# Batch 0's job list of an attention + gated-FFN kernel in another order, and the last pair of x turned by DMA

## The chip, the cores and the metric

The kernel runs on one core of a Trainium2 chip. The core has five engines that work side by side, each through its own list of instructions in order: TensorE (PE, matmuls; its weight loads, PEld, overlap them), VectorE (DVE), ScalarE (ACT), GpSimd (POOL) and SyncE (SP, which here only issues DMAs). An instruction that needs another engine's result waits at the head of its list, and everything behind it on that engine waits too. The metric is the device time of one execution in microseconds (us).

## What is computed

Four batches of eight heads, 768 tokens, head size 64. Queries and keys are hashed by the signs of six projections; a query attends only to keys with the same hash. The output of the attention, with the heads side by side, is x (3072 x 512), and x goes through a gated FFN with a residual.

```python
q_bits = einsum('bhsd,dk->bhsk', q, proj) > 0          # the same for k
mask = q_bucket[:, :, :, None] == k_bucket[:, :, None, :]
attn = softmax(where(mask, q @ k.T / sqrt(D), -1e9))
x = (attn @ v).transpose(0, 2, 1, 3).reshape(B * S, H * D)
out = x + sigmoid(x @ w_res) * ((gelu(x @ w_gate) * (x @ w_val)) @ w_out)
```

## The kernel before

**Pairs and slots.** Two heads form a pair (p = 0 to 15, four to a batch). A pair's scores are computed in nine slots; a slot (`scores`, L535) is three or two matmuls into a PSUM tile of 1024 columns, `sp` (two buffers), and one exp of 128x1024 on ScalarE (L553). Two slots later, or where the list says so, `values` (L506) multiplies by v, eight matmuls (L515), into `av`. When a head is done, `finish` (L458) divides by the sum on VectorE (L466, L467) and writes x with the tokens on the partitions, `x_tok`. The FFN needs x the other way round, `x_sb`, in four quarters, one a pair. A quarter is turned either by a DMA transpose that SP issues (L470), or on TensorE by `x_turn` (L496): six transposes into PSUM (L499) and copies to `x_sb` by ScalarE and VectorE (L501 to L504).

**The hash inside the matmul.** The six signs stand beside the 64 numbers of each query and key in one row of 71, so that the matmul itself lets only equal hashes through. For that each pair's q and k go through these steps, named here as in the list: `ld` loads it (SP), `tr` transposes it on VectorE (L265), `h` multiplies it by the projections on TensorE (L283, several pairs in one group, four steps: h10 to h13 are group 1, pairs 2 and 3), `tk` turns a group's results on VectorE (L303), `bt` takes the signs (L319; for k of pairs 1 to 3 two of its four instructions are on GpSimd, two on VectorE), `cs` casts the numbers to bf16 beside them on GpSimd (L223 for q, L225 for k), and then either `tp` turns the rows on TensorE, six transposes to a head (L384), with `td` copying them out on VectorE (L393), or `tu` turns them by one DMA transpose (L372). In a name like tp310 the digits are pair, side (0 is q, 1 is k) and head. There are four tiles `nat` for the rows, one for each side of two pairs, and two PSUM banks for turns and hashes.

**v** is loaded by `lv`, cast on GpSimd by `va` (L432, L433) and summed there by `vs` (four instructions, L440 to L444).

**Weights.** `w0` to `w11` each issue one DMA of a slice of the FFN's weights from GpSimd (L208): four times gate and val by turns, then the residual's, then three of the output's. The issue itself occupies GpSimd.

**What sets the order.** Nothing is scheduled by a tool: the order in which the program emits its pieces is the order of every engine. For batch 0 a list written out by hand, `ORDER` (L20), gives it: s and v are the slots' scores and values, fin a `finish`, xt an `x_turn`; the job names are bound to functions in L716 to L766. `FIRST_LOADS` (L17) gives the first loads on SP. Ahead of the list stand fixed pieces for pair 0 and the casts of pair 1 (L626 to L655), among them the cast of pair 1's q, va(0), the cast of pair 1's k and the spreading of the projections over `projw`, in this order on GpSimd. The list ends where x of batch 0 is complete. `BESIDE` (L31) names the jobs that are emitted behind each of the twelve steps m of batch 0's FFN stage (`gate_val`, L570): a step is eight matmuls for gate and eight for val (L566), Gelu on ScalarE (L583) and their product on VectorE (L586). From pair 4 on the jobs are placed by slot numbers (L681 to L826), and the rest of the FFN (`project`, L592: for each of six token blocks four row matmuls by w_res and twelve by w_out, 96 in all, L598 and L614) is spread over the next batch's 36 slots by `mlp_mm` (L831, L851). `HELD`, 16, of them are kept back for the end of a batch, where they fill the time in which x is turned (L857 to L872). In batches 1 and 2 all four quarters of x are turned by DMA; in batch 0 the last two, and in batch 3 the last one, on TensorE.

## Time and profile before

| what | value |
|---|---|
| median of 3 runs | 340.84 us (340.73 to 341.19) |
| the profiled execution's own time | 340.31 us |
| its span, first to last instruction | 338.6 us |
| mean granted TensorE clock | 1.000 |
| busy: PE, DVE, ACT, POOL | 333.2, 216.9, 206.2, 171.9 us |
| first exp of batch 0 | 7.80 us |
| end of batch 0's 36 exps | 44.99 us |
| its FFN stage (gate and val matmuls) | 48.4 to 80 us |
| batches 1 to 3 in slots | 80 to 280 us |
| last batch's FFN stage | 280 us to the end |

In a row of a timeline stand the start, the length of the group, the engine, the line, the operation with out<-in by the program's names, the shapes and a count; in brackets how long the engine was idle before it, and what ended that. A row can hold several instructions, and a length of TensorE is modelled and reaches into the next row, so that one reads such lengths from start to start. Rows of a window (A:B) give the sum of all engines and then PE, PEld, DVE, ACT and POOL, each busy time with its count, the granted clock, the DMA engines' busy share, and GB/s. The chain of work that ended last names at each moment what the end of the program hung on.

### The profile page before, as it was taken

Reading aid. Unit: us, or ns where it says so; the run is one execution under the profiler, and the core shown is the slowest. Engines: PE = TensorE matmul, PEld = TensorE weight load, DVE = VectorE, ACT = ScalarE, POOL = GpSimd, SP = SyncE. Lnnn points to the kernel's source line nnn. Section 1 sums busy time; section 2 is a strip of 40 time slices with the busy share of each in tenths; the row PEclk is TensorE's granted clock in tenths of the full one; section 3 lists DMA queues with packets and bytes.
Section 4 is the critical chain, followed back from the end, with each engine's and each line's share of the span. In section 5 each row is a group of like instructions: output and inputs, shape, how many; then the busy total and the mean of one; then the engine's idle time right before and its main releaser. Section 6 shows DMA issues by size and latency. Waiting matters only on the chain.

```text
span 338.6 us, 7598 instructions
## 1 busy us (share of the span) xinstructions
PE 333.2 (98%) x3058; PEld 203.1 (60%) x3058; DVE 216.9 (64%) x418; ACT 206.2 (61%) x232; POOL 171.9 (51%) x220
## 2 busy tenths in 40 slices
PE   8999999999999999999999999999999999999995
PEld 4667766655666655655666665656566665666444
DVE  6889457574445748888887766887897444343343
ACT  4889963317999952235999982233999984223220
POOL 5879920410665306998999704998998000000000
PEclk9999999999999999999999999999999999999999
DMA  7997897799876634350488832551261420000012
GB/s 211 379 249 169 160 252 128 132 190 199 240 164 187 207 94 99 73 96 0 126 219 204 277 106 62 102 96 28 48 148 39 97 56 33 31 0 2 31 64 94
DMA packets 71459, 43.09 MB, mean 127 GB/s; under 512 B 49536, under 2 KB 68480, under 8 KB 71424
## 3 DMA queue, kind: packets, MB, share of 16 engines
q1 hardware_dynamic: 65008, 37.37, 43.7%
q0 software_dynamic: 6336, 5.24, 10.1%
q8 instruction: 24, 0.39, 0.5%
q14 instruction: 11, 0.09, 0.1%
q10 hardware_dynamic: 80, 0.00, 0.0%
HBM read 29.56 MB, written 6.29 MB: 106 GB/s over the span
## 4 chain that ended last, share of the span: by engine, by line
PE 91%; ACT 4%; DVE 3%; issue 1%; DVEq 0%; ACTq 0%
PE sp L566 35%; PE fps L614 18%; PE sp L542 17%; PE av L515 9%; PE rps L598 6%; ACT hh L553 4%; PE hs L283 2%; DVE hh L586 1%; PE wps L189 1%; PE pt L384 1%; PE hs L330 1%; DVE nat L319 1%; DVE hsum L361 0%; PE pt L499 0%; DVE o L621 0%
## 5 line engine op out<-in xcount | busy, mean ns | idle before, releaser
L553 ACT ACTIVATE e<-sp 128x1024 bf16<-128x1024 f32 x108 | 109.0, 1028 | 8.1 <-PE sp L542 2.8
L357 POOL TENSOR_TENSOR pd<-ld,prow 128x768 f32<-128x768 f32 x48 | 86.1, 1811 | 36.8 <-PE hs L283 32.6
L583 ACT ACTIVATE gt<-sp 128x768 bf16<-128x768 f32 x48 | 38.9, 810 | 89.8 <-PE sp L566 89.8
L542 PE MATMUL sp<-aug,aug 71*128 71x256 bf16 (+1 forms) x384 | 85.5, 325 | 0.1
L614 PE MATMUL fps<-wo,hh 128*128 128x512 bf16 (+2 forms) x312 | 79.5, 362 | 0.0
L566 PE MATMUL sp<-x_sb,wv 128*128 128x512 bf16 (+1 forms) x384 | 70.9, 326 | 0.4 <-DVE hh L586 0.4
L566 PE MATMUL sp<-x_sb,wg 128*128 128x512 bf16 (+1 forms) x384 | 70.9, 326 | 0.1
L586 DVE TENSOR_TENSOR hh<-gt,sp 128x768 bf16<-128x768 bf16 x48 | 45.8, 954 | 39.0 <-PE sp L566 34.2
L515 PEld LDWEIGHTS <-e 128*128 128x128 bf16 x864 | 40.2, 97 | 25.1
L566 PEld LDWEIGHTS <-wv 128*128 128x128 bf16 x384 | 37.6, 98 | 25.5 <-issue 0.8
L566 PEld LDWEIGHTS <-wg 128*128 128x128 bf16 x384 | 36.9, 98 | 25.8 <-issue 1.7
L361 DVE TENSOR_REDUCE hsum<-pd 128x12 f32<-128x768 f32 x48 | 44.4, 943 | 0.5
L515 PE MATMUL av<-va,e 128*128 128x65 bf16 x864 | 43.4, 193 | 0.0
L614 PEld LDWEIGHTS <-hh 128*128 128x128 bf16 x312 | 28.1, 97 | 21.8
L553 ACT ACTIVATE hh<-sp 128x1024 bf16<-128x1024 f32 x36 | 34.5, 1024 | 3.4 <-PE sp L542 3.0
L542 PEld LDWEIGHTS <-aug 71*128 71x128 bf16 x384 | 29.5, 97 | 11.0 <-issue 1.1
L617 DVE SCALAR_TENSOR_TENSOR fps<-th,fps 128x512 f32<-128x512 f32 (+2 forms) x26 | 16.9, 650 | 28.3 <-PE fps L614 27.8
L598 PE MATMUL rps<-wr,x_sb 128*128 128x512 bf16 x96 | 27.1, 379 | 0.0
L494 DVE COPY av<-av 128x390 f32<-128x390 f32 x24 | 13.7, 571 | 19.6 <-PE av L490 19.6
L602 ACT ACTIVATE th<-rps 128x512 f32<-128x512 f32 x24 | 14.3, 594 | 18.5 <-PE rps L598 18.5
L223 POOL TENSOR_SCALAR nat<-ld 128x768 bf16<-128x768 f32 (+1 forms) x16 | 13.0, 813 | 18.6 <-DMA aug<-nat 18.0
L265 DVE STREAM_TRANSPOSE t<-ld 128x768 f32<-128x768 f32 (+1 forms) x24 | 21.9, 925 | 0.1
(77 smaller groups left out, 259.6 us busy)
## 6 DMA issues: line engine op xcount, KB each, us to landing
ldv<-in_v_dram SPq DMA_DIRECT2D x16, 384.0 KB, 5.1
out_dram<-o SPq DMA_DIRECT2D x23, 256.0 KB, 2.0
ld<-in_q_dram SPq DMA_DIRECT2D x15, 384.0 KB, 5.6
ld<-in_k_dram SPq DMA_DIRECT2D x15, 384.0 KB, 6.0
wg<-in_moe_w_gate_dram POOLq DMA_DIRECT2D x4, 384.0 KB, 9.1
wv<-in_moe_w_val_dram POOLq DMA_DIRECT2D x4, 384.0 KB, 11.8
wo<-in_moe_w_out_dram POOLq DMA_DIRECT2D x3, 512.0 KB, 11.8
wr<-in_moe_w_res_dram POOLq DMA_DIRECT2D x1, 512.0 KB, 7.7
```

What stands on the lines that cost most here:

```text
L265: nc.vector.transpose(t32[p, side][:, sl].rearrange("p c h n -> p (c h n)"), raw[p, side][:, sl].rearrange("p c d -> p (c d)"))
L357: nc.gpsimd.tensor_mul(pd, raw[x], prow[:, j].unsqueeze(1).to_broadcast([P, HT, D]))
L361: nc.vector.tensor_reduce(stripes(hsum6)[:, :, :, j], hparts.pop((x, j)).rearrange("p (a c) d -> p a c d", a=3), axis=mybir.AxisListType.X ...
L515: nc.tensor.matmul(av[p, hi][:, qt, :], e[:, off:off + P], va[:, hi, jt, 0:D + 1], start=first, stop=(p >= HP and jt == T - 1), skip_group ...
L542: nc.tensor.matmul(sp[:, off:off + nq * P], ks[0:KA, hi * T + jt, :], qs[0:KA, hi * T + qt0:hi * T + qt0 + nq, :], start=True, stop=True)
L553: nc.scalar.activation(e, sp, AF.Exp, scale=float(ALPHA))
L566: nc.tensor.matmul(sp[:, c0:c1], w[:, kk, bass.ts(m, P)], xs[:, kk, c0:c1], start=(kk == 0), stop=(kk == KM - 1))
L583: nc.scalar.activation(gt, sp[:, 0:S], AF.Gelu)
L586: nc.vector.tensor_mul(hidden[b][:, m, :], gt, ps[1][:, 0:S])
L598: nc.tensor.matmul(rps, x_sb[b][:, kk, t, :], wr[:, kk, :], start=(kk == 0), stop=(kk == KM - 1))
L614: nc.tensor.matmul(fps[:, cs], hh[:, m, bass.ts(t, P)], wo[:, m, cs], start=(m == 0), stop=(m == KF - 1))
L617: nc.vector.scalar_tensor_tensor(fps[:, cs], th[:, cs], 1.0, fps[:, cs], op0=ALU.add, op1=ALU.mult)
```

## The change

Two things are changed. The first is batch 0's list: `FIRST_LOADS`, `ORDER` and `BESIDE` hold the same jobs in another order (a few pass from one of the lists to another).

```diff
-FIRST_LOADS = [(1, "q"), (0, "v"), (1, "k"), (2, "q"), (2, "k"), (2, "v"), (3, "q"), (3, "k"), (1, "v")]
+FIRST_LOADS = [(0, "v"), (1, "q"), (1, "k"), (2, "q"), (2, "k"), (2, "v"), (1, "v"), (3, "q"), (3, "k")]
...
 ORDER = """
-trq tpB tdk tdq trk s0 hoq tr10 ld50 s1 bo0 s2 ho bo1 tp001 td001 s3 tp011 td011a ld40 tr11 ld51 v0
-v1 cs21 td011b s4 s5 h00 h01 h02 h03 tr20 s6 s7 v2 v3 v4 tk0 bt10 bt11 tp100 tp110 td100 td110 tr21
-s8 tr30 tr31 tp111 td111 cs31 s9 tp101 td101 s10 w0 v5 v6 v7 v8 s11 cs20 s12 ld61 fin00 ld41 h10 h11
-w1 s13 h12 h13 fin01 cs30 s14 lv3 ld70 s15 va1 v9 v10 v11 s16 tk1 bt20 bt21 bt31 tp200 tp210 td200
-td210 vs1 s17 tp211 td211 cs41 tr50 s18 tp201 td201 va2 s19 tp310 vs2 s20 vs3 bt30 td310 v12 v13 s21
-v14 fin10 s22 tp300 tr40 w2 tp301 s23 v15 tr51 s24 lv4 va4 v16 v17 s25 v18 s26 v19 v20 v21 td301
-td300 s27 fin11 v22 s28 cs50 tp311 s29 ld71 v23 fin20 w3 w4 s30 lv5 w5 v24 v25 td311 s31 v26 fin21
-va3 tr41 v27 s32 w6 v28 v29 v30 s33 xt2 s34 v31 s35 gelu tr61 v32 v33 v34 g0 v35 fin30 op40 g1 fin31
-xt3 ld60 h20 h21 h22 w7
+trq tpB tdq s0 tdk trk hoq bo0 ho bo1 s1 tr10 tr11 lv3 s2 tp011 td011a tp001 v0 td001 v1 s3 td011b
+cs21 h00 h01 s4 tr20 s5 ld40 h02 h03 s6 v2 v3 v4 cs20 s7 tr21 tk0 bt10 bt11 tp100 tp110 td100 td110
+ld50 s8 ld51 fin00 tp111 tr30 ld41 s9 tp101 td101 vs2 s10 tr31 v5 v6 v7 v8 fin01 s11 td111 s12 h10
+va2 h11 h12 h13 s13 s14 va1 v9 v10 v11 v12 s15 tk1 bt20 bt21 tp210 td210 vs1 cs30 s16 tp200 td200
+ld60 w0 w1 w2 va3 bt30 s17 v13 v14 vs3 tr40 s18 tp211 cs41 td211 s19 v15 v16 s20 fin10 tp201 lv4 s21
+bt31 cs31 va4 v17 v18 td201 s22 tp301 td301 s23 ld61 tp300 td300 s24 tp310 tr50 fin11 cs40 v19 ld70
+s25 v20 v21 vs4 lv5 s26 td310 s27 v22 tr61 s28 tr41 v23 v24 v25 s29 tp311 td311 cs51 fin20 s30 v26
+cs50 s31 v27 tr51 s32 w3 v28 v29 v30 s33 fin21 xt2 s34 lv6 v31 v32 fin30 op40 s35 v33 v34 g0 gelu
+v35 fin31 w4 w5 w6 g1 xt3 h20 h21 h22 tr60
 """
 BESIDE = [
-    "vs4 lv6 cs40 h23 tk2 bt41",
-    "cs51 bt50",
-    "tu50 cs70 tr70",
-    "bt40 tu40 cs60 w8 w9 w10 w11",
-    "bt51",
-    "tr71",
-    "tu51",
-    "tr60",
-    "h30 h31 h32 tu41 cs61 h33 tk3 bt60 bt61 tu60 tu61",
-    "cs71 bt71 tu71",
-    "bt70 tu70",
-    "pr40 rp40",
+    "h23 tk2 bt41",
+    "bt50 tu50",
+    "bt40 tu40 cs60",
+    "bt51 w7",
+    "pr40 rp40 tu41 cs61",
+    "tr70",
+    "ld71 tr71 w8 w9 w10",
+    "",
+    "",
+    "tu51 cs71 h30 h31 h32 h33 tk3 bt60 bt61 tu61 cs70",
+    "bt70 tu70 bt71",
+    "w11 tu60 tu71",
 ]
```

The second is at the end of batch 3. The last quarter of x is turned by a DMA transpose, issued in `finish` as for batches 1 and 2, and no longer by `x_turn`. `HELD_LAST`, 20, row matmuls are kept back there instead of 16: one less is emitted at slots 18, 24, 30 and 35 of the last batch. Of the 20, four come ahead of the last values (as before), ten (nine before) behind the first gate and val matmuls, three between the last quarter's matmuls of step 0 and its product (as before), and three behind that product.

```diff
-        if hi == 1 and (0 < b < B - 1 or hp < HP - (X_PE if b == 0 else 1)):
+        if hi == 1 and (b > 0 or hp < HP - X_PE):
             nc.sync.dma_start_transpose(out=x_sb[b][:, hp],
...
     HELD = 16
+    HELD_LAST = 20
...
-        mlp_mm(AHEAD + (slot + 1) * (NMM - HELD - AHEAD) // NSLOT - done[0])
+        held_back = (HELD_LAST - HELD) * (b == B - 1) * max(0, slot - 12) // (NSLOT - 1 - 12)
+        mlp_mm(AHEAD + (slot + 1) * (NMM - HELD - AHEAD) // NSLOT - held_back - done[0])
...
             else:
-                x_turn(b, HP - 1)
-                mlp_mm(HELD - 7)
+                mlp_mm(HELD_LAST - 10)
                 gv(b, 0, lambda: mlp_mm(NMM))
                 gate_val(b, begun, lambda: mlp_mm(3))
```

## The prediction

> **What bounds the kernel now.** I read the page first, then ScalarE's, GpSimd's and TensorE's timelines from 7 to 50 us, then all engines from 277 us on. The time is 340.31 us for the profiled execution: a span of 338.6 and 1.7 around it.

> ```profile
> span 338.6 us, 7598 instructions
> PE 333.2 (98%) x3058; PEld 203.1 (60%) x3058; DVE 216.9 (64%) x418; ACT 206.2 (61%) x232; POOL 171.9 (51%) x220
> PE 91%; ACT 4%; DVE 3%; issue 1%; DVEq 0%; ACTq 0%
> L553 ACT ACTIVATE e<-sp 128x1024 bf16<-128x1024 f32 x108 | 109.0, 1028 | 8.1 <-PE sp L542 2.8
> ```

> TensorE carries the chain nearly everywhere; the 4% of ScalarE lie in one place. In batch 0's attention (7.8 to 45 us) 36 exps of 1.02 us stand back to back:

> ```profile
> 7.80 4.15 ACT L553 ACTIVATE hh<-sp 128x1024 bf16<-128x1024 f32 x4 [0.68 <-PE sp L542]
> 12.39 1.94 ACT L553 ACTIVATE hh<-sp 128x1024 bf16<-128x1024 f32 x2 [0.44 <-PE sp L542]
> 14.79 1.94 ACT L553 ACTIVATE hh<-sp 128x1024 bf16<-128x1024 f32 x2 [0.46 <-PE sp L542]
> 17.46 2.85 ACT L553 ACTIVATE hh<-sp 128x1024 bf16<-128x1024 f32 x3 [0.73 <-PE sp L542]
> 20.80 2.86 ACT L553 ACTIVATE hh<-sp 128x1024 bf16<-128x1024 f32 x3 [0.49 <-PE sp L542]
> 23.90 21.09 ACT L553 ACTIVATE hh<-sp 128x1024 bf16<-128x1024 f32 x22 [0.24 <-PE sp L542]
> 24.00:45.00 21.00, 20.91 (x327) 16.10 (x326) 15.26 (x37) 20.82 (x22) 19.73 (x36) 1.00 0.87 179
> ```

> The reader is to see three things. Before 23.9 us ScalarE waits for scores five times, 2.36 us in all after the first exp. From 23.9 on it runs 22 exps without a gap. And in the last row (sum, PE, PEld, DVE, ACT, POOL) GpSimd is busy 19.73 of 21 us in the same stretch: a third engine has no slack there. GpSimd waits in order and feeds TensorE, since a turn of a pair's q or k on TensorE (tp) reads what GpSimd cast (cs).

> **Batch 0's list: what moves on GpSimd.** No job is added; the new list only orders them anew. Between tk1 and tp310 the old list gives GpSimd little that tp310 needs: cs31, the cast of pair 3's k, ran long before.

> ```profile
> 17.88 0.82 POOL L225 CAST nat<-ld 128x768 bf16<-128x768 f32 x1 [1.81 <-PE pt L384]
> 28.28 0.50 PE L384 MATMUL pt<-ident,nat 128*71 128x128 bf16 x6
> ```

> It began at 17.88, tp310 at 28.28. The new list has cs31 behind tk1, bt21, vs1, cs30, the weight loads w0, w1, w2, va3, vs3, cs41 and bt31. GpSimd reaches bt21 and must stop there, because bt21 reads what VectorE turns in tk1; all the rest stands behind it. Each of these jobs has a row in the old run; I time them from start to start:

> ```profile
> 23.40 0.58 DVE L303 STREAM_TRANSPOSE ht<-hs 128x384 f32<-128x384 f32 x1 [0.81 <-PE hs L283]
> 24.14 2.06 POOL L319 TENSOR_SCALAR nat<-ht 32x72 bf16<-32x72 f32 x4 [1.15 <-DVE ht L303]
> 26.28 0.99 POOL L440 TENSOR_TENSOR v<-ldv 128x384 f32<-128x384 f32 x1
> 28.32 0.83 POOL L225 CAST nat<-ld 128x768 bf16<-128x768 f32 x1
> 29.09 0.83 POOL L432 CAST va<-ldv 128x768 bf16<-128x768 f32 x1
> 29.92 1.00 POOL L440 TENSOR_TENSOR v<-ldv 128x384 f32<-128x384 f32 x1
> 37.33 0.75 POOL L208 DMA_DIRECT2D wg<-in_moe_w_gate_dram  x1
> 38.06 0.76 POOL L208 DMA_DIRECT2D wv<-in_moe_w_val_dram  x1
> 18.65 0.98 POOL L208 DMA_DIRECT2D wg<-in_moe_w_gate_dram  x1
> ```

> Four bits operations take 26.28 - 24.14 = 2.14, so bt21's or bt31's two 1.07; a vs 28.32 - 26.28 = 2.04; a cast 29.09 - 28.32 = 0.77; a va 29.92 - 29.09 = 0.83; a weight issue 38.06 - 37.33 = 0.73. The chain is 1.07 + 2.04 + 0.77 + 3 x 0.73 + 0.83 + 2.04 + 0.77 + 1.07 + 0.83 (cs31 to its end) = 11.6 us.

> Where it starts: tk1 waits for hash matmul h13. The new list holds TensorE up early. q1's load goes out one place later, which is about 1.04 us (384 KB at 379 GB/s, the first row below), so GpSimd's first full cast, at 8.74 before, starts between 8.74 and 9.78; I take 9.3, and projw near 11.75 instead of 11.18. h00 needs projw's four copies, 0.87 us, so it can go at about 12.65; it now stands ahead of s4 and s5, and TensorE, done with s3 near 11.95, waits there some 0.7 us where it had scores to do.

> ```profile
> 8.46:16.90 8.44, 8.35 (x105) 5.77 (x104) 7.00 (x18) 7.20 (x8) 7.03 (x17) 1.00 1.07 379
> 8.74 0.83 POOL L223 TENSOR_SCALAR nat<-ld 128x768 bf16<-128x768 f32 x1
> 11.18 0.87 POOL L183 COPY projw<-projn 32x12 f32<-32x12 f32 x4
> 14.15 1.04 PE L542 MATMUL sp<-aug,aug 71*128 71x512 bf16 x5
> 22.40 0.86 PE L283 MATMUL hs<-t,projw 128*32 128x192 f32 x16
> ```

> The old run is through s5 and h03 at 14.15. The new one gets there 0.9 later: the 0.7, and 0.2 to 0.3 for v0, whose va(0) waits in the same row of casts. By h13 the new list has s13 still ahead of it, which the old one had done: 0.43 comes off. The waits of turns on VectorE and GpSimd (tp100, tp110, tp101), 0.2 to 0.3 in all, are spent while TensorE is late anyway. So h13 ends near 23.4 against 23.26, and tk1 starts at 23.6 against 23.40; as bounds I take 22.8 (no loss early, and s13's 0.43 saved) and 24.4 (the whole 0.9). Then bt21 starts 0.74 behind tk1's start, as in the rows, at 24.35; cs31 ends at 24.35 + 11.6 = 35.95; **tp310 starts near 36.1**.

> Who waits: a score slot takes TensorE 0.43, so s13 ends at 23.85; the next eleven follow at ScalarE's pace, (2.85 - 1.02) / 2 = 0.92 by the row at 17.46, and s24 ends near 34.0. TensorE then stands still for about 2 us. Queued behind tp310 on TensorE are v19 and s25, and behind s25 every remaining exp.

> ```profile
> 33.65 0.60 PE L542 MATMUL sp<-aug,aug 71*128 71x256 bf16 x3
> 34.08 0.41 PE L515 MATMUL av<-va,hh 128*128 128x65 bf16 x8
> 34.34 0.71 ACT hh L553
> 39.61 0.41 PE L515 MATMUL av<-va,hh 128*128 128x65 bf16 x8
> 39.85 0.33 PE L487 MATMUL av<-vsum,eps_sb 128*128 128x390 bf16 x1
> 281.87 0.50 PE L499 MATMUL pt<-ident,x_tok 128*128 128x128 bf16 x6
> 282.21 2.11 PE L614 MATMUL fps<-wo,hh 128*128 128x512 bf16 x9
> 48.40:80.00 31.60, 31.49 (x226) 18.70 (x223) 21.49 (x48) 10.10 (x13) 6.27 (x8) 1.00 0.98 160
> ```

> Six turns take 282.21 - 281.87 = 0.34, a slot's scores 34.08 - 33.65 = 0.43, a v 39.85 - 39.61 = 0.24, and s25's start to its exp 34.34 - 33.65 = 0.69. The new exp 25 starts at 36.1 + 0.34 + 0.24 + 0.69 = 37.37 instead of 34.34: 3.0 us late. From there to the end of exp 35 the old run takes 44.99 - 34.34 = 10.65; at the pace of 0.92 it is 10 x 0.92 + 1.02 = 10.2, so 0.4 comes back: TensorE, with 0.43 of scores, 0.24 to 0.31 of values and some 0.1 of turns a slot, does not hinder that. **Batch 0 ends 2.6 us later.** Behind exp 35 the list does the same work in the same order (v35, fin31, g1, xt3), so all of it moves on into the FFN stage, where TensorE has no gap in which it could be made up (31.49 of 31.60 us busy from 48.4 to 80).

> What the new order does to ScalarE's early gaps neither costs nor brings anything by itself: cs31 sets the time, and it hangs on tk1 alone.

> [...]

> **The rest of the list, costed at nothing.** ld71 is now issued in the FFN stage behind three turns by DMA on SP; tr71 on VectorE needs it in m=6, 10 us behind tu40. If it lands late, hh of m=7 and TensorE's m=8 wait as long. w8 to w11 are issued 5 to 7 us later; the wo slice that w11 loads is read about 7 us into batch 1's slots. Medians from issue to landing are 6.0 and 11.8 us, so the margins are some 2 and 3 us. pr40 and rp40 move to m=4, 0.6 us of VectorE beside 2.6 us of TensorE a step.

> ```profile
> ld<-in_k_dram SPq DMA_DIRECT2D x15, 384.0 KB, 6.0
> wo<-in_moe_w_out_dram POOLq DMA_DIRECT2D x3, 512.0 KB, 11.8
> ```

> **The last pair of x.** Removed: six turns on TensorE, 281.87 to 282.21, and the two copies. Added: one DMA transpose on SP. Four row matmuls of 0.216 move from the slots to behind them; their sum stays.

> ```profile
> 280.35 0.56 DVE L467 TENSOR_TENSOR x_tok<-av,rec 128x384 bf16<-128x384 f32 x1
> DMA to landing us min/median/max: 2.7/2.8/6.4
> 280.00:338.60 58.60, 55.08 (x333) 30.91 (x329) 22.73 (x34) 15.45 (x21) 0.00 (x0) 1.00 0.10 37
> ```

> x_tok is done at 280.91, the transpose lands 2.8 later at 283.7. TensorE does 10 rows from 281.87, to 284.03, before it reads the last quarter of x: 0.3 us of cover. So the turns' **0.34 us is gained**. SP is free, since the o of the row before is now written behind finish. With the slowest landing, 6.4, the wait would be 287.3 - 284.0 = 3.3; it decides from 3.1 on. The slow landings lie in batch 0, among the loads; here nothing but an output row moves (DMA share 0.10 in the last row), so 2.8 is the nearest.

> **Sum.** 340.31 + 2.6 - 0.34 = 342.6 for an execution like the profiled one, which was 0.53 below the median of the runs; against that, 340.84 + 2.3 = **343.1 us**.

> **Rivals.**
> - *The order pays.* If GpSimd's chain ran through ahead of s25, the 2.36 us of ScalarE's early gaps could close: 340.84 - 2.36 - 0.34 = 338.1. For it: from 7.8 to 45 us those gaps are all the time in which ScalarE has nothing to do. Against it: 11.6 us of GpSimd work from 24.35 on, with TensorE free at 34.0. It decides where the chain is under 9.6 us. Chance 0.09.
> - *The chain is shorter* (GpSimd's spans are rough, tk1 starts at 22.8, more than 0.4 comes back behind exp 25), so that nearly nothing or up to 1.4 us is lost net: 340.2 to 342.2. Chance 0.14, 0.09 of it within 0.2%.
> - *A second wait*: the last x lands late, ld71 or w11 does, or the three issues take 0.98: 344.4 to 346.5. Chance 0.16.
> - *The clock falls in the wait.* If TensorE ran at half speed for some us after its stop, four slots of some 0.8 would take 1.6 each against ScalarE's 0.92, 2.7 us more: 345.8. The granted clock is 1.00 in every stretch and no stop of 2 us is in the old trace. Chance 0.03. [...]

> The forecast has 0.58, 342.2 to 344.4 (tk1's bounds, and 0.3 either way in what comes back). The range, 341.0 to 345.4, leaves out the first rival, 0.06 of the second, and 0.04 at the far end of the last two. What a measurement of this kernel can tell from no change is about 0.2%, 0.7 us: faster by more 0.09, within it 0.09, slower 0.82.

> **What would show it.** On TensorE a stop of about 2 us ahead of tp310, ended by GpSimd's cast L225 near 36 us, and one gap of ScalarE ahead of exp 25 where there is none now. The table load for Gelu, 45.00 now, near 47.6. At the end no L499 turns, and the last quarter of x read with no wait behind an x transpose landing in 2.8 us. Wrong, if cs31 ends before 34 us, or if TensorE stops in the FFN stage for ld71's tr71 or a weight.

## The result, and the profile after

| | before | after |
|---|---|---|
| median of 6 runs, us | 341.03 (340.73 to 341.63) | 349.85 (346.82 to 350.89) |
| profiled execution, us | 340.31 | 346.82 |
| mean granted clock | 1.000 (profiled) | 0.995 (profiled), 0.985 (four runs), 0.980 (one) |

After takes 1.0246 times as long, 95% interval 1.0208 to 1.0285. The kernel is slower, as forecast, but by 8.8 us and not by 2.3. The profiled execution is the fastest of the six: it lost 6.5 us against the profiled one of before, the others lost 8.3 to 9.9 against the median of before, at a lower mean clock. Two things are therefore asked: where do the 6.5 us lie, and what makes the runs differ.

From the page of after, the span, the busy times, the clock granted in 40 slices (tenths), and the chain that ended last by engine:

```profile
span 345.1 us, 7583 instructions
PE 334.6 (97%) x3052; PEld 203.5 (59%) x3052; DVE 216.6 (63%) x417; ACT 205.7 (60%) x231; POOL 171.8 (50%) x220
PEclk9999899999999999999999999999999999999999
PE 86%; POOL 4%; DVE 4%; DMA 2%; issue 1%; SPq 1%; ACT 1%; DVEq 0%; POOLq 0%; ACTq 0%
```

GpSimd, which was not in the chain before, now has 4% of it, and one slice, 34.5 to 43.1 us, shows a clock under full. TensorE's timeline of after there, and the row of its waits:

```profile
33.48 0.59 PE L542 MATMUL sp<-aug,aug 71*128 71x512 bf16 x2
38.44 0.85 PE L384 MATMUL pt<-ident,nat 128*71 128x128 bf16 x6 [4.36 <-POOL nat L225]
39.09 0.65 PE L515 MATMUL av<-va,hh 128*128 128x65 bf16 x8
39.54 1.04 PE L542 MATMUL sp<-aug,aug 71*128 71x256 bf16 x3
...
43.24 0.59 PE L542 MATMUL sp<-aug,aug 71*128 71x256 bf16 x3 [0.33 <-ACT hh L553]
```

The stop stands where it was forecast: s24 ends at 34.08, and tp310 waits for cs31, GpSimd's cast L225. It lasts 4.36 us, not 2. Behind it the same three score matmuls take 1.04 at 39.54 and 0.59 at 43.24. ScalarE's timeline gives what that costs:

```profile
23.93 11.33 ACT L553 ACTIVATE hh<-sp 128x1024 bf16<-128x1024 f32 x12 [0.47 <-PE sp L542]
40.68 1.02 ACT L553 ACTIVATE hh<-sp 128x1024 bf16<-128x1024 f32 x1 [5.42 <-PE sp L542]
42.16 9.67 ACT L553 ACTIVATE hh<-sp 128x1024 bf16<-128x1024 f32 x10 [0.45 <-PE sp L542]
51.85 1.28 ACT L765 ACT_TABLE_LOAD   x1
```

The Gelu table load, the end of batch 0's exps, stands at 51.85 instead of 45.00: 6.85 later. From it to the end of the span there are 345.1 - 51.85 = 293.25 us, before 338.6 - 45.00 = 293.6. So batch 0 lost 6.85 us and the rest gained 0.35: the whole loss lies ahead of 51.85.

GpSimd's timeline of after shows why cs31 is late:

```profile
24.18 0.97 POOL L319 TENSOR_SCALAR nat<-ht 32x72 bf16<-32x72 f32 x2 [3.21 <-DVE ht L303]
27.30 0.83 POOL L223 TENSOR_SCALAR nat<-ld 128x768 bf16<-128x768 f32 x1
30.21 0.98 POOL L208 DMA_DIRECT2D wg<-in_moe_w_gate_dram  x1 [2.08 <-issue]
37.56 0.83 POOL L225 CAST nat<-ld 128x768 bf16<-128x768 f32 x1
```

bt21 begins at 24.18 (forecast 24.35). But between cs30's end, 28.13, and the first weight issue, w0, GpSimd does nothing for 2.08 us and waits for nothing that the profile shows ("issue"). cs31 ends at 38.39 and not at 35.95.

So three things have to be told apart: the stop; an idle of 2 us on GpSimd ahead of w0, with an unknown cause; and a clock halved behind the stop. The rivals are the other parts of the change, and another cause for the spread.

### The profile page after: what moved, and what is told of

Same layout as the page of the kernel before. It is cut to its first block, busy times and chain, and to the rows that moved or that the text cites. A ratio compares the mean times of both kernels' runs of the same rounds, so it can differ in the third digit from the quotient of the medians.

```text
span 345.1 us, 7583 instructions
## 1 busy us (share of the span) xinstructions
PE 334.6 (97%) x3052; PEld 203.5 (59%) x3052; DVE 216.6 (63%) x417; ACT 205.7 (60%) x231; POOL 171.8 (50%) x220
## 4 chain that ended last, share of the span: by engine, by line
PE 86%; POOL 4%; DVE 4%; DMA 2%; issue 1%; SPq 1%; ACT 1%; DVEq 0%; POOLq 0%; ACTq 0%
PE sp L566 34%; PE fps L614 18%; PE sp L542 16%; PE av L515 9%; PE rps L598 6%; PE hs L283 2%; DMA ld<-in_k_dram 1%; DVE hh L586 1%; DMA ld<-in_q_dram 1%; POOL nat L225 1%; DVE aug L393 1%; DVE nat L319 1%; DVE t L265 1%; POOL wg L208 0%; POOL va L432 0%
## 5 line engine op out<-in xcount | busy, mean ns | idle before, releaser
L553 ACT ACTIVATE e<-sp 128x1024 bf16<-128x1024 f32 x108 | 108.8, 1028 | 7.8 <-PE sp L542 2.8
L542 PE MATMUL sp<-aug,aug 71*128 71x256 bf16 (+1 forms) x384 | 85.9, 327 | 0.4 <-ACT hh L553 0.3
L614 PE MATMUL fps<-wo,hh 128*128 128x512 bf16 (+2 forms) x312 | 79.6, 362 | 0.0
L515 PEld LDWEIGHTS <-e 128*128 128x128 bf16 x864 | 40.2, 97 | 25.0
L566 PEld LDWEIGHTS <-wv 128*128 128x128 bf16 x384 | 37.6, 98 | 25.5 <-issue 0.8
L566 PEld LDWEIGHTS <-wg 128*128 128x128 bf16 x384 | 36.9, 98 | 25.6 <-issue 1.5
L515 PE MATMUL av<-va,e 128*128 128x65 bf16 x864 | 43.4, 193 | 0.0
L614 PEld LDWEIGHTS <-hh 128*128 128x128 bf16 x312 | 28.2, 97 | 22.1
L553 ACT ACTIVATE hh<-sp 128x1024 bf16<-128x1024 f32 x36 | 34.5, 1024 | 10.4 <-PE sp L542 10.2
L542 PEld LDWEIGHTS <-aug 71*128 71x128 bf16 x384 | 29.6, 98 | 11.4 <-issue 2.3
L617 DVE SCALAR_TENSOR_TENSOR fps<-th,fps 128x512 f32<-128x512 f32 (+2 forms) x26 | 16.9, 649 | 25.9 <-PE fps L614 25.1
L223 POOL TENSOR_SCALAR nat<-ld 128x768 bf16<-128x768 f32 (+1 forms) x16 | 13.0, 811 | 18.4 <-DMA aug<-nat 17.7
## 6 DMA issues: line engine op xcount, KB each, us to landing
ldv<-in_v_dram SPq DMA_DIRECT2D x16, 384.0 KB, 4.8
ld<-in_q_dram SPq DMA_DIRECT2D x15, 384.0 KB, 4.7
ld<-in_k_dram SPq DMA_DIRECT2D x15, 384.0 KB, 5.6
wg<-in_moe_w_gate_dram POOLq DMA_DIRECT2D x4, 384.0 KB, 6.6
wv<-in_moe_w_val_dram POOLq DMA_DIRECT2D x4, 384.0 KB, 6.5
wo<-in_moe_w_out_dram POOLq DMA_DIRECT2D x3, 512.0 KB, 10.3
wr<-in_moe_w_res_dram POOLq DMA_DIRECT2D x1, 512.0 KB, 8.7
```

What stands on the lines that cost most here:

```text
L515: nc.tensor.matmul(av[p, hi][:, qt, :], e[:, off:off + P], va[:, hi, jt, 0:D + 1], start=first, stop=(p >= HP and jt == T - 1), skip_group ...
L542: nc.tensor.matmul(sp[:, off:off + nq * P], ks[0:KA, hi * T + jt, :], qs[0:KA, hi * T + qt0:hi * T + qt0 + nq, :], start=True, stop=True)
L553: nc.scalar.activation(e, sp, AF.Exp, scale=float(ALPHA))
L566: nc.tensor.matmul(sp[:, c0:c1], w[:, kk, bass.ts(m, P)], xs[:, kk, c0:c1], start=(kk == 0), stop=(kk == KM - 1))
L614: nc.tensor.matmul(fps[:, cs], hh[:, m, bass.ts(t, P)], wo[:, m, cs], start=(m == 0), stop=(m == KF - 1))
L617: nc.vector.scalar_tensor_tensor(fps[:, cs], th[:, cs], 1.0, fps[:, cs], op0=ALU.add, op1=ALU.mult)
```

## The experiments

There are eleven experiments; two of them, e8 and e11, are after and e5 once more. Ratios are to the kernel before, run on the same chip in the same series (medians 341.03, 340.91 and 340.89).

### The cast ahead of the weight issues, and the weight issues behind the cast

```diff
-tk1 bt20 bt21 tp210 td210 vs1 cs30 s16        # e1
+tk1 bt20 bt21 tp210 td210 vs1 bt31 cs31 cs30 s16
...
-ld60 w0 w1 w2 va3                             # e2
+ld60 va3
-bt31 cs31 va4
+bt31 cs31 w0 w1 w2 va4
```

> The new kernel with bt31 and cs31 moved in the list to directly behind vs1, ahead of cs30 and of w0, w1, w2. Theory (TensorE stops ahead of tp310 for cs31 at the end of GpSimd's chain, and the stop halves the granted clock for 3.4 us): cs31 ends near 28.1 us of the profile, well before tp310 is reached at about 34, so no stop of more than 0.5 us stands ahead of tp310, the mean granted clock is 1.000, the Gelu table load comes back from 51.85 us to 45 to 46, and the time is 340 to 341.5 us. Rival (the new hold-back in the last batch, the work beside the expert weights' stage or the loads there cost the time): the time stays at 345 us or more, with the table load at 45 to 46 us and a later stage longer. If an idle of about 2 us still stands on GpSimd ahead of the first weight issue, it is there but harmless.

> The new kernel with w0, w1, w2 moved in the list from behind ld60 to behind cs31. Theory a (the 2.08 us of idle ahead of w0 belong to the issue itself): the idle moves with w0 behind cs31, cs31 ends at about 38.39 - 2.08 - 3 x 0.75 = 34.1 us, TensorE stops under 0.7 us ahead of tp310, the clock stays 1.000 and the time is 340.3 to 341.5 us. Theory b (the idle belongs to the place in GpSimd's stream or to the moment): it stays behind cs30, cs31 ends at about 36.2 us, TensorE stops about 2.1 us, the time is 342.3 to 343 us at clock 1.000, or 344 to 345 if a stop of 2 us is enough to halve the clock. Rival (the stop at tp310 isn't what costs): 346 to 350 us.

e1: 340.92 us, ratio 0.9995 (0.9983 to 1.0007). e2: 341.37, ratio 1.0004 (0.9991 to 1.0017). All 24 runs have a clock of 0.998 or more. In neither profile does TensorE wait for a cast there. ScalarE in e1, and then GpSimd:

```profile
23.81 21.86 ACT L553 ACTIVATE hh<-sp 128x1024 bf16<-128x1024 f32 x23 [0.47 <-PE sp L542]
45.69 1.28 ACT L765 ACT_TABLE_LOAD   x1
```

```profile
31.29 0.98 POOL L208 DMA_DIRECT2D wg<-in_moe_w_gate_dram  x1 [1.33 <-issue]
```

GpSimd in e2:

```profile
32.84 0.82 POOL L225 CAST nat<-ld 128x768 bf16<-128x768 f32 x1
33.61 0.98 POOL L208 DMA_DIRECT2D wg<-in_moe_w_gate_dram  x1
```

Moving one cast with its bits (bt31, cs31), or three issues, by a few places gives back the whole loss, so it hangs on this chain alone and the other parts of the change cost next to nothing. In e1 the idle ahead of w0 is there (1.33) and harmless. In e2, where the issue comes later, it is not there at all: cs31 ends at 33.66, before TensorE asks for it, 0.4 earlier than I had expected. So the idle isn't a price of the first weight issue as such, which was theory a of e2 (its time came true, its reason did not), and it didn't stay behind cs30 either, which was theory b. What is left of the loss is early: the load stands at 45.69 instead of 45.00, with the last-x part's gain against it.

### The two halves of the change apart

> The kernel before with the last batch's part of the change alone: x of the last pair by DMA transpose, twenty row matmuls held back there, the old lists. Theory: the six turns go (-0.34 us), nothing waits for the transpose, 340.5 to 340.8 us at a clock of 1.000. Rival (the tail costs): 341.5 us or more, with an idle of TensorE ahead of the gate matmul of the last x block.

> The new kernel with the old end of the last batch (six turns, sixteen row matmuls held back), the new lists kept. Theory: the whole loss is in the list, so the time is that of the new kernel plus 0.34 us, 347 to 351 us, with the stop of 4.4 us ahead of tp310 and a half-clock window behind it. Rival (the tail costs): 341 to 343 us.

e3 is the kernel before with the last batch's part of the diff alone, e4 the kernel after without it. e4: 349.02 us, ratio 1.0218 (1.0186 to 1.0251), with the stop and the half clock of after; the list holds the loss. e3: 341.25, ratio 1.0004 (0.9989 to 1.0019), above the 340.5 to 340.8 that I had expected: 0.34 is less than the runs can tell. Its profiled execution, 341.74, was hit by something else, and not by the rival's wait in the last batch: TensorE waits once in batch 1 for a sum of v by GpSimd:

```profile
92.08 0.19 PE L490 MATMUL av<-vsum,eps_sb 128*128 128x65 bf16 x1 [1.24 <-POOL vsum L444]
```

From the Gelu load to the end the profiles tell it better. e4's load, in a span of 345.1 us:

```profile
51.37 1.28 ACT L764 ACT_TABLE_LOAD   x1
```

That leaves 293.7 with the old ending, 293.6 in before; with the new one 293.25 in after and 293.2 in e1. So, by one profile each, the ending gains about 0.45 (e4 against after), and the later weight issues and `BESIDE` cost about 0.1 (e4 against before). In the last batch of after, SP and then TensorE:

```profile
287.09 1.22 SPq L470 DMA_TRANSPOSE x_sb<-x_tok  x1
```

```profile
288.89 1.46 PE L614 MATMUL fps<-wo,hh 128*128 128x512 bf16 x6
290.18 0.49 PE L566 MATMUL sp<-x_sb,wg 128*128 128x512 bf16 x2
```

The six row matmuls follow each other, and the two gate matmuls that read the last quarter of x start behind them at 290.18 without a wait. That part of the change does what it says.

### GpSimd's idle: twelve small instructions

```diff
-tk1 bt20 bt21 tp210
+tk1 bt20 pad bt21 tp210
...
+    def pad():
+        for _ in range(12):
+            nc.gpsimd.memset(padt, 0.0)
```

> The new kernel with twelve memsets of a spare 128x2 tile on GpSimd ahead of its half of bt21, where GpSimd waits 3.2 us for VectorE anyway; nothing else is changed. [...] Theory b (the idle belongs to the first weight issue in that stretch, or to VectorE's work at 28 to 30 us): it stays at about 2 us and the time at 346 to 351 us.

Asked is whether the idle ahead of w0 stays when GpSimd has twelve instructions more ahead of bt21. It does not, and theory b falls. GpSimd, TensorE and ScalarE in e5:

```profile
23.80 0.97 POOL L319 TENSOR_SCALAR nat<-ht 32x72 bf16<-32x72 f32 x2 [1.39 <-DVE ht L303]
26.92 0.83 POOL L223 TENSOR_SCALAR nat<-ld 128x768 bf16<-128x768 f32 x1
27.70 0.98 POOL L208 DMA_DIRECT2D wg<-in_moe_w_gate_dram  x1
```

```profile
35.94 0.53 PE L384 MATMUL pt<-ident,nat 128*71 128x128 bf16 x6 [2.17 <-POOL nat L225]
```

```profile
37.24 10.60 ACT L553 ACTIVATE hh<-sp 128x1024 bf16<-128x1024 f32 x11 [2.29 <-PE sp L542]
47.86 1.28 ACT L772 ACT_TABLE_LOAD   x1
```

More work on GpSimd, and cs31 ends 2.5 us earlier. The idle is gone, the stop is 2.17, tp310 starts at 35.94. In the DMA view, q14 is a queue that the profile calls instruction (its packets, MB, share). Between 24 us and w0, after has two of them, which begin in the trace at 25.94 and 28.36. In windows of 0.1 us, 25.9 to 26 and 28.3 to 28.4:

```profile
q14 instruction: 1, 0.01, 52.1%
q14 instruction: 1, 0.01, 19.3%
```

The last two ahead of w0 in e5 begin at 20.05 and 25.59. Its windows 20 to 20.1 and 25.5 to 25.6:

```profile
q14 instruction: 1, 0.01, 20.1%
q14 instruction: 1, 0.01, 23.8%
```

In every kernel that has the idle, w0 starts nearly the same time behind the later packet: 30.21 - 28.36 = 1.85 in after, 1.84 in e4, 1.86 in e1, 1.75 in e6 and e7, 1.85 in e8, 1.82 in e10. In e5 the nearest packet is 2.1 us ahead of w0, and there is no idle. The trace does not name the engine that a packet is for. The packet at 25.59 in e5 stands 1.79 us behind bt21's start, and the one at 25.94 in after 1.76: if these two are the same, the one that moved with the memsets is the other, from 28.36 to 20.05. Either way e5 has no packet in the 1.85 us ahead of w0. What the idle is, no row shows: the profile calls it "issue", and e2 has such a packet at 28.73 with no idle behind it. VectorE's work at that moment, which theory b names too, need not hold up an issue: in before w0 went at 18.65 with no idle ahead of it (its row stands in the prediction), in the middle of three transposes of VectorE:

```profile
17.61 2.70 DVE L265 STREAM_TRANSPOSE t<-ld 128x768 f32<-128x768 f32 x3
```

The median, 344.58 (ratio 1.0110, 1.0061 to 1.0160), is a mixture: three runs of 342.69 to 343.36 at a clock of 1.000, one of 345.80 at 0.990, two of 347.4 at 0.985.

### The clock: TensorE kept at work

```diff
-td300 s24 tp310
+td300 s24 busy tp310
...
+    def busy():
+        t = mm_ps.tile([P, 512], FP32, tag=take(), name="wps2")
+        for _ in range(18):          # 9 in e9, which also has the pad of e5
+            nc.tensor.matmul(t, ones(P), ones(512), start=True, stop=True)
```

> The new kernel with eighteen matmuls of ones (128x512) into a spare bank ahead of tp310, so that TensorE works some 3.9 us through the stop; it still waits for cs31 there. Theory (the idle window halves the clock, and the spread between runs is the number of half-clock windows that follow): the mean granted clock is 1.000 in every run, exp25 follows tp310 by 1.2 to 1.4 us instead of 2.24, the time is 346.8 - 1.9 = 344.9 us (344.4 to 345.4), and the runs lie within 1 us of each other as those of the kernel before do. Rival (the loss behind the stop and the spread have another cause): 346.5 to 351 us, clock 0.98 to 0.995.

> The kernel of e5 (twelve memsets on GpSimd, so that no idle stands ahead of w0 and TensorE's stop at tp310 is about 2.2 us) with nine matmuls of ones (128x512, about 2.05 us) ahead of tp310, so that TensorE works through the stop. Theory (the runs of e5 at 345.8 to 347.4 us are those in which a window of 3.41 us held enough of the stop to halve the clock): every run has a clock of 0.999 or more and takes 342.5 to 343.5 us, spread about 1 us. Rival (another stop, or GpSimd's idle coming back in some runs): a part of the runs stays at 345 us or more.

TensorE and ScalarE in e6:

```profile
34.53 4.10 PE L768 MATMUL wps<-const-bfloat16-1.0 128*128 128x512 bf16 x18
39.34 0.53 PE L384 MATMUL pt<-ident,nat 128*71 128x128 bf16 x6 [0.71 <-POOL nat L225]
```

```profile
40.64 10.60 ACT L553 ACTIVATE hh<-sp 128x1024 bf16<-128x1024 f32 x11 [4.76 <-PE sp L542]
51.26 1.28 ACT L771 ACT_TABLE_LOAD   x1
```

tp310 starts 0.9 later than in after (the start of the program took 0.6 more, the idle ahead of w0 was 2.35), and yet the Gelu load is 0.6 earlier. Exp 25 follows tp310 by 1.30 instead of 2.24, and the load follows exp 25 by 10.62 instead of 11.17: one half-clock window cost 0.94 + 0.55 = 1.5 us. The two profiles of one kernel with the memsets, e5 at full clock and e11 (below) with one half-clock window, give the same: 1.30 against 2.24 and 10.62 against 11.18. The clock is 0.999 or more in all five runs, 345.42 to 346.85 us, median 346.23 (ratio 1.0146, 1.0118 to 1.0174): matmuls that compute nothing make it faster than after by 3.6 us, and by 2.2 against the runs of after in the same series (e8, below). The runs lie within 1.4 us of each other. The time is 1.3 above what I had expected, which is 0.9 for the later tp310 and 0.4 for a price of the window set at 1.9.

e9, with both causes gone, takes 343.36 us (342.87 to 343.80, ratio 1.0074, 1.0060 to 1.0088), its runs within 0.9 us (expected 342.5 to 343.5). That is the forecast stop and nothing else.

### How long a stop halves the clock

> The new kernel with bt31 and cs31 one place earlier on GpSimd, ahead of cs41 instead of behind it, so that the stop at tp310 ends about 0.8 us earlier (some 3.5 us instead of 4.36). Theory a (the clock falls when one whole window of 3.41 us is idle, and in the profile of the new kernel the windows are 35.03 to 38.44 and 31.6 to 35.0): no window is idle as a whole, the clock stays 1.000 and the time is 346.82 - 0.8 - 1.9 = 344.1 us. Theory b (any stop over some 3.4 us halves it): 346.0 us at 0.995, or more where further windows follow. Rival (the length of the stop doesn't set the time): 349 us.

> The new kernel once more, for more runs of its clock and another profile. Theory: the time goes with the mean granted clock: one half-clock window of 3.41 us (0.995) with 346.8 us, two (0.99) with about 348.6, three (0.985) with 349.3 to 350.2, four (0.98) with 350.9; they follow the stop at tp310 without a break.

> The new kernel with 28 memsets of a spare 128x2 tile on GpSimd ahead of bt31 (0.15 us each, 4.2 us), so that the stop at tp310 lasts about 8.6 us instead of 4.36. Theory a (half-clock windows that fall into the stop cost nothing, and a window of work at half clock ends it): 346.8 + 4.2 = 351.0 us in every run, up to 352.5 where two windows of work stand behind the stop. Theory b (a longer stop keeps the clock down for longer): 353 us or more, with three or more half-clock windows behind the end of the stop.

> The kernel of e5 once more (stop of about 2.2 us at tp310), for more runs and another profile. Theory: the place of the stop against the windows of 3.41 us differs from run to run; where a window holds no more than some 0.4 of its length of idle, the clock stays 1.000 and the time is 342.7 to 343.4 us; where it holds more (up to 2.2 of 3.41 us, 0.64), the clock is halved for one to three windows, 345 to 347.5 us. A profile at 0.985 would show the window ahead of the drop between 0.4 and 0.64 idle.

```diff
-tp211 cs41 td211 ... bt31 cs31 va4            # e7
+tp211 bt31 cs31 cs41 td211 ... va4
...
-bt31 cs31 va4                                 # e10: slow is 28 memsets on GpSimd
+slow bt31 cs31 va4
```

In after the granted clock changes at 38.26 and 41.67 us, 34.13 and 37.55 behind its first entry at 4.12: ten and eleven times 3.413 us. Rows cut every 3.413 us about the stop in e7, e10 and e11 read 1.00 or 0.50 too, and nothing between. So a window of this grid can be read as one row: its length, then PE's busy time first, and the clock behind the five engines. The windows about the stop in after, where TensorE was idle for the whole of the one ahead of the drop (the expectation for e7 had put that one at 35.03 to 38.44):

```profile
34.84:38.26 3.42, 0.00 (x0) 0.00 (x0) 0.80 (x3) 0.42 (x1) 3.10 (x7) 1.00 1.32 203
38.26:41.67 3.41, 3.23 (x34) 2.58 (x35) 2.30 (x3) 0.99 (x1) 3.25 (x7) 0.50 1.15 326
```

The same in e7, whose stop is 3.95 us (I had expected 3.5; the idle ahead of w0 was 2.45):

```profile
32.44:35.85 3.41, 1.49 (x14) 0.74 (x11) 2.63 (x5) 2.74 (x3) 3.25 (x7) 1.00 1.20 154
35.85:39.27 3.42, 1.33 (x16) 1.27 (x17) 0.43 (x1) 0.00 (x0) 3.18 (x7) 0.50 1.31 207
39.27:42.68 3.41, 3.41 (x28) 2.13 (x27) 1.86 (x3) 1.78 (x2) 2.92 (x7) 0.50 1.12 329
42.68:46.09 3.41, 3.41 (x39) 2.50 (x37) 0.00 (x0) 2.20 (x3) 0.00 (x0) 0.50 0.16 56
```

And in e11 and then e5, which are one kernel with the same stop of 2.17 us:

```profile
32.64:36.05 3.41, 1.35 (x11) 0.68 (x9) 2.72 (x5) 2.60 (x3) 3.09 (x7) 1.00 1.32 204
36.05:39.47 3.42, 3.24 (x34) 2.57 (x35) 2.30 (x3) 1.00 (x1) 3.26 (x7) 0.50 0.92 178
```

```profile
31.32:34.73 3.41, 2.38 (x28) 1.51 (x24) 2.12 (x4) 3.41 (x4) 3.08 (x7) 1.00 1.31 203
34.73:38.15 3.42, 2.13 (x36) 1.69 (x37) 2.25 (x5) 1.13 (x2) 3.35 (x6) 1.00 1.01 156
```

In e11 the stop lies in one window, which is busy for 1.35 of 3.41, 60% idle, and the next window runs at half clock. In e5 the window's edge cuts the stop, the two windows are 30% and 38% idle, and the clock stays. e7's window of 1.49, 56% idle, also brought the drop: theory a of e7, that a whole window must be idle, falls, and so does b, since 2.17 us can suffice. In these traces, whose TensorE lengths are modelled, the point lies between 38% and 56% of a window. By that, e7's second half-clock window needs no other cause, since the first, 35.85 to 39.27, was itself 61% idle; the third does, since the second was busy throughout.

e11's median is 345.91 us (342.95 to 347.12, ratio 1.0145, 1.0108 to 1.0181). The twelve runs of the two go with it: at 1.000 four of 342.69 to 343.36, at 0.995 two of 344.65 and 345.17, at 0.990 two of 345.80 and 346.65, at 0.985 four of 346.80 to 347.42. One half window in 341 us is 0.5 x 3.413 / 341 = 0.005 of the mean, so these are none, one, two and three windows. e7: 347.97 us (346.85 to 349.67, ratio 1.0203, 1.0169 to 1.0236), two or three windows in each run, and so above theory a's 344.1 and above the 346.0 that theory b gave for one window; the runs of e7 and e8 are too near each other to show what 0.4 us less of a stop is worth. e8, the kernel after again: 348.43 (347.11 to 350.66, ratio 1.0220, 1.0176 to 1.0263), 0.985 to 0.995; its profile shows one window again. Time and clock go together only roughly: its run at 0.990 took 347.35, where I had expected 348.6.

e10: 354.17 us (352.62 to 354.98, ratio 1.0386, 1.0365 to 1.0408). TensorE stops 9.21 us, 0.6 more than I had expected, with two half-clock windows inside the stop and one behind it in the profiled run:

```profile
43.98 0.85 PE L384 MATMUL pt<-ident,nat 128*71 128x128 bf16 x6 [9.21 <-POOL nat L225]
```

```profile
44.31:47.72 3.41, 3.41 (x36) 2.61 (x35) 2.30 (x3) 1.02 (x1) 3.15 (x7) 0.50 0.00 0
```

That is 346.82 + 4.85 for the longer stop, 351.7, and 0.9 over, of which 0.7 is a later start (its exp of after's 23.93 stands at 24.62): theory a, for this run. The four other runs, at 0.976 to 0.980, are 1.2 to 2.4 us above, 353.83 to 354.98, so theory a's "every run" failed, and these times lie where theory b had put them; no profile shows where their further windows lie.

## Why the prediction was wrong, point by point

- **Which wait, and where.** Right. TensorE stops ahead of tp310 for the cast cs31; s24 ends at 34.08 (forecast 34.0); beside the early wait for projw (0.5 us, forecast 0.7) nothing else of the list stops TensorE for more than 0.3 us in batch 0's attention.
- **The chain's start.** Right: bt21 at 24.18 and, in e5, 23.80, against 24.35.
- **The chain's length, 11.6 us.** Its jobs take 12.1: in e5 from 23.80 to cs31's end at 35.89, of which the three weight issues are 2.47 instead of 2.19 (the first takes 0.98, the others 0.75). This failed first: in after the chain takes 38.39 - 24.18 = 14.2 us, because GpSimd stands idle for 2.08 us ahead of w0. The sum was made of job lengths, and no row of before shows such an idle in this stretch.
- **tp310 at 36.1, exp 25 at 37.37.** Without the idle (e5): 35.94 and 37.24. In after: 38.44 and 40.68.
- **0.4 comes back behind exp 25.** It didn't. From exp 25 to the Gelu load are 10.66 us in before and 10.62 in e5 at full clock, and 11.17 in after. I had put the pace at 0.92 a slot; e5's eleven exps take 10.60 in a row, 0.96 each.
- **The clock.** This failed most. I gave it 3% and 345.8, since the old trace had no stop of 2 us. The price was too high for one window (1.5 measured, 2.7 forecast) and the chance far too low: at the very stop that I forecast, 2.17 us, it falls in eight of twelve runs, and at 4.36 in every one. In five of the six runs of after it falls for three windows or more (a mean of 0.985 or 0.980). A window of 3.41 us that was 56% (e7) or 60% idle (e11) was enough. The grid of these windows begins at 4.12 us of the span in after and, counted back from the rows above, at 4.02 in e5, 5.14 in e7 and 6.77 in e10, another place in each run.
- **The rest of the list at nothing, the last x at 0.34.** Right: about 0.1 and 0.45.
- **Three weight issues at 0.98, in the second wait.** No run shows them: of the three issues the first takes 0.98 in after, e2 and e5 alike, and the two behind it 0.75 each, 2.47 together in e5.

So the forecast of 343.1 us is the kernel without the two effects: e9 measures 343.36. That it is met so closely is in part luck: in e5 the chain is 0.5 us longer than forecast and 0.4 doesn't come back, against a start 0.55 earlier and 0.1 more gained at the end. The idle adds 2.9 (e6 against e9, both at full clock; 2.4 by their profiles), and the half clock 2.2 to 3.6 (e8 and after against e6). What of this is open: why the clock stays down for one window in some runs and three in others, although in e7 TensorE was busy for the whole of 39.27 to 42.68; and what the idle ahead of w0 is: a packet of the instruction queue stands 1.75 to 1.86 us ahead of w0 in all seven profiles that have the idle, but the one at 28.73 in e2 holds up neither va3, whose last instruction starts at 28.77, nor the sum of v behind it, at 28.84.

## What to carry to other kernels

Time a chain on an engine that waits in order by its jobs, but leave room for an idle that no job explains: here an idle of 2.08 us ahead of a DMA issue on GpSimd stood in front of a cast that TensorE waited for, so casts on which matmuls hang go ahead of such issues (e1, e2). A stop of TensorE cost more than its length here: the clock halved behind a window of 3.41 us that was 56% idle and stayed at 38%. Behind a stop of 2.17 us it fell in eight of twelve runs, and that showed as a spread between runs with different mean clocks. Where a stop can't be moved, matmuls of ones through it are worth trying: here they gave back 2.2 to 3.6 us.
